# First loads spread over two hardware queues, the cast queue started later, half of a batch's q turned by DMA: one change to an attention and feed-forward kernel

## The chip, the core and the metric

One core of a Trainium2 chip. The metric is the device time of one execution in microseconds (us). Most executions of this kernel agree within 0.3%, and the change is worth about that much, so the timed runs are read together with traces, which resolve single instructions.

## The reference

```python
# q [8,16,384,64]; k, v [8,4,384,64]; 4 q heads share one k, v head (a "group")
scores = q @ k^T / sqrt(64)
attn   = softmax(scores) @ v
x      = attn with the heads side by side      # [3072, 1024]
h      = max(x @ w_in, 0)                      # w_in  [1024, 2048]
out    = (h * h) @ w_out                       # w_out [2048, 1024]
```

## The kernel before

The program records operations with a planned cost, and a loop picks for TensorE (PE) at each step what its own model says is ready. The order of instructions is thus fixed when the program is built; on the chip the engines follow it and wait by semaphores. Batches are called b0 to b7. To turn q, k or an attention output is to transpose it. A burst is the score matmuls and the one exp that reads them; the small exps are the 20 of b0. The cast queue is the DMA queue of gpsimd, whose loads turn f32 into bf16. While ScalarE (ACT) does the exps of one batch, PE fills in with the feed-forward of the batch before.

The parts that matter, with cuts marked:

```python
def first_loads():                       # f32, hardware queues
    for g0, g1 in ((0, 1), (1, HKV)):
        R.add("sync",   ... k_f32 groups g0..g1 ...)        # small k, then the bulk of k
    for n in range(2):
        R.add("scalar", ... q_f32 heads 2n, 2n+1 ...)       # both q loads on the other queue
...
def turn_q_dma(b, half):                 # transposes 8 of 16 heads by DMA, 384 KB
    R.add("sync", lambda e: e.dma_start_transpose(out=qT[b % 2][...], in_=q_st[b % NST][...]),
          ..., dma=f"turn_q{half}", cost=2.5, shared=8.0)
def turn_q_pe(b, g, banks, t0=0, t1=6):  # the same on PE: 6 transposes a group, then a DVE copy
    ...
# the cast queue (gpsimd), one long queue in this order:
load_q(0, 4, 8); ...identity...; load_v(0); load_q(0, 8, 12); load_q(0, 12, 16); load_w_in(0)
load_k(1); load_q(1, 0, 8); load_q(1, 8, 16); load_w_in(1); load_v(1)
load_w_in(2) ... load_w_in(7)
load_w_out(0, 0); load_w_out(0, 1); load_w_out(1, 0); load_w_out(1, 1)    # 1 MB each as read
# then k, q, v of b2
...
warm_up(22, 2.5)        # matmuls on zeros until the first k is there
...
# loop: turn_q = b0 and b1 on PE; from b2 on, k and q are turned by DMA
if turn_q and (b == 0 or pairs < 6 or x_done[0] == 8): ...   # candidate "turn"
```

The down projection of b0 uses the four w_out blocks in the order (0, 0), (0, 1), (1, 0), (1, 1). Each output tile of the first half starts with 8 matmuls from block (0, 0), then 8 from block (0, 1). I call (0, 1) the second block; its first use is the ninth w_out matmul of the program.

The softmax here doesn't subtract the row's maximum and nothing guards it: scores larger than these inputs give would overflow.

## Time and profile before

| | before |
|---|---|
| timed, first 3 runs | 430.74 us median (430.25 to 430.86) |
| profiled execution, span | 428.1 us |
| first exp on ACT | 6.59 us |
| first w_out matmul, ninth w_out matmul | 53.14 us, 54.87 us |
| second w_out block landed (landing events of the trace) | 49.84 us |

First the page of the kernel before: the span, the busy time of each engine, the clock that the record grants PE by fortieths of the span (9 is full), and the chain of work that ended last.

```profile
span 428.1 us, 7844 instructions
...
PE 423.2 (99%) x3467; PEld 232.2 (54%) x3467; DVE 158.8 (37%) x334; ACT 194.9 (46%) x194; POOL 55.1 (13%) x67
...
PEclk8999999999999999999999999999999999999999
...
PE 98%; DMA 1%; ACT 0%; DVE 0%; ACTq 0%; issue 0%
```

PE bounds the kernel. The Trainium skill ("Perfetto Trace Analysis", Identifying the Most-Contended Engine) says that the busy share of matmuls is no good measure of how close a kernel is to its limit, because pipelined instructions look smaller in the trace, and asks for the share of peak arithmetic and the busy share of weight loads instead; weight loads are at 54% here, so 99% is not "99% of the peak". For a kernel like this I read the starts of successive matmuls: a start later than the columns of the one before explain is time that PE lost. Some matmul records are missing from a few of the traces below; such a hole is one matmul long (0.22 us for a matmul of 512 columns) and is not a wait.

Next the timeline of the kernel before at its start: start, duration, engine, line, operation, tiles, count, and in brackets the engine's idle time before it with the releaser.

```profile
4.52 0.41 PE L302 MATMUL ps<-ident,q_st 128*128 128x128 bf16 x3
4.96 0.36 DVE L309 COPY qT<-ps 128x384 bf16<-128x384 bf16 x1 [0.38 <-PE ps L302]
5.30 0.51 ACT L551 CAST q_st<-q_f 128x384 bf16<-128x384 f32 x1 [0.97 <-DMA q_f<-in_q_dram]
5.96 0.33 PE L302 MATMUL ps<-ident,q_st 128*128 128x128 bf16 x3 [1.03 <-ACT q_st L551]
6.22 0.34 PE L328 MATMUL ps<-qT,kT 64*128 64x384 bf16 x2
6.59 2.43 ACT L338 ACTIVATE expT<-ps 128x768 bf16<-128x768 f32 x3 [0.78 <-PE ps L328]
...
9.81 0.82 PE L302 MATMUL ps<-ident,q_st 128*128 128x128 bf16 x6
...
11.43 0.52 PE L302 MATMUL ps<-ident,q_st 128*128 128x128 bf16 x6
```

ACT waits for the second q load until 5.30 us, PE stands for the second three transposes until 5.96, and the first score (L328) is behind them. The last two lines show the clock: six such transposes take 0.82 us at 9.81 and 0.52 us at 11.43. The table by stretches says the same in its column PEclk (here 0.52 of full between 8 and 10 us; the columns are busy time by engine with instruction counts, PEclk, DMA share, GB/s):

```profile
core 0: us, PE busy (x) PEld busy (x) DVE busy (x) ACT busy (x) POOL busy (x), PEclk, DMA share, GB/s
...
8.00:10.00 2.00, 2.00 (x17) 0.78 (x15) 0.92 (x2) 2.00 (x4) 2.00 (x4) 0.52 1.45 182
```

### The profile page before, as it was taken

The numbers are of one execution on the slowest core, as the hardware profiler recorded it, in microseconds if no ns is written. First come the engines' busy times: TensorE is split into PE (matmuls) and PEld (weight loads), VectorE is DVE, ScalarE is ACT, GpSimd is POOL, SyncE is SP. The second block draws the span as 40 slices with busy tenths as digits, with TensorE's granted clock in tenths as the row PEclk, the third lists the DMA queues.
The fourth block names the chain that finished last, engine by engine and source line by source line (L and its number), as shares of the span: only waits on it lengthen the run. The fifth ranks groups of instructions, "written<-read, shape, count | busy, mean of one in ns | idle before, by whom it ended". The sixth has DMA issues, their size and how long they took to land.

```text
span 428.1 us, 7844 instructions
## 1 busy us (share of the span) xinstructions
PE 423.2 (99%) x3467; PEld 232.2 (54%) x3467; DVE 158.8 (37%) x334; ACT 194.9 (46%) x194; POOL 55.1 (13%) x67
## 2 busy tenths in 40 slices
PE   7999999999999999999999999999999999999997
PEld 5565554565445654456554465645564465446544
DVE  2674432254223542325432253523342144214412
ACT  6947740557545675446765459550230033003300
POOL 8680011413040022004000000000000000000000
PEclk8999999999999999999999999999999999999999
DMA  9999999999599179369647410032001100110012
GB/s 180 193 198 204 187 195 190 236 152 130 90 188 166 20 133 141 98 145 145 64 80 140 89 45 18 16 92 81 37 2 49 73 26 2 49 73 26 1 66 83
DMA packets 95347, 43.90 MB, mean 103 GB/s; under 512 B 75728, under 2 KB 89296, under 8 KB 95312
## 3 DMA queue, kind: packets, MB, share of 16 engines
q0 software_dynamic: 36544, 17.44, 32.4%
q1 hardware_dynamic: 58224, 25.57, 28.0%
q8 instruction: 27, 0.44, 0.4%
q10 hardware_dynamic: 544, 0.39, 0.3%
q14 instruction: 8, 0.07, 0.1%
HBM read 35.65 MB, written 12.58 MB: 113 GB/s over the span
## 4 chain that ended last, share of the span: by engine, by line
PE 98%; DMA 1%; ACT 0%; DVE 0%; ACTq 0%; issue 0%
PE ps L431 40%; PE ps L480 39%; PE ps L374 9%; PE ps L349 7%; PE ps L328 1%; DMA q_f<-in_q_dram 1%; PE ps L302 1%; PE ps L407 0%; PE ps L286 0%; ACT expT L338 0%; DVE o_sb L389 0%; ACT q_st L551 0%; ACTq L218 0%; DVE y_sb L489 0%; DVE rinv L383 0%
## 5 line engine op out<-in xcount | busy, mean ns | idle before, releaser
L431 PE MATMUL ps<-xT,w_in_sb 128*128 128x384 bf16 x1024 | 175.0, 326 | 0.0
L480 PE MATMUL ps<-w_out_sb,h2T 128*128 128x512 bf16 (+2 forms) x784 | 172.0, 375 | 0.0
L359 ACT ACTIVATE expT<-ps 128x3072 bf16<-128x3072 f32 x42 | 114.4, 2725 | 57.7 <-PE ps L349 57.1
L431 PEld LDWEIGHTS ps<-xT,w_in_sb 128*128 128x128 bf16 x1024 | 96.8, 98 | 69.2 <-issue 6.4
L441 ACT ACTIVATE h2T<-hr 128x384 bf16<-128x384 f32 x128 | 64.3, 520 | 148.8 <-DVE hr L439 148.7
L480 PEld LDWEIGHTS ps<-w_out_sb,h2T 128*128 128x128 bf16 x784 | 73.8, 98 | 87.6 <-issue 5.4
L439 DVE TENSOR_SCALAR hr<-ps 128x384 f32<-128x384 f32 x128 | 71.1, 557 | 104.8 <-PE ps L431 104.8
L489 DVE COPY y_sb<-ps 128x512 f32<-128x512 f32 (+2 forms) x49 | 33.4, 681 | 127.4 <-PE ps L480 127.4
L374 PEld LDWEIGHTS ps<-v_aug,expT 128*128 128x128 bf16 x1152 | 39.8, 97 | 6.6 <-DVE o_sb L389 0.7
L374 PE MATMUL ps<-v_aug,expT 128*128 128x65 bf16 x1152 | 41.6, 193 | 0.1
L389 DVE TENSOR_TENSOR o_sb<-ps,rinv 128x384 bf16<-128x384 f32 x64 | 35.7, 558 | 2.2
L349 PE MATMUL ps<-qT,kT 64*128 64x512 bf16 (+1 forms) x336 | 34.6, 325 | 0.0
L349 PEld LDWEIGHTS ps<-qT,kT 64*128 64x128 bf16 x336 | 13.0, 94 | 20.7 <-issue 5.4
L383 DVE RECIPROCAL rinv<-ps 128x6 f32<-128x6 f32 x64 | 12.2, 190 | 24.1 <-PE ps L374 24.0
L338 ACT ACTIVATE expT<-ps 128x1024 bf16<-128x1024 f32 (+1 forms) x20 | 17.2, 941 | 1.7 <-PE ps L328 1.5
L263 POOL COPY v_aug<-v_st 128x768 bf16<-128x768 bf16 x8 | 6.7, 832 | 87.0 <-PE ps L374 71.9
L258 POOL COPY k_dup<-k_st 128x1536 bf16<-128x1536 bf16 x7 | 10.3, 1467 | 36.7 <-DMA k_st<-in_k_dram 36.7
L231 POOL DMA_DIRECT2D q_st<-in_q_dram x17 | 14.9, 888 | 0.9 <-POOLq L726 0.8
L205 POOL DMA_DIRECT2D k_st<-in_k_dram x7 | 5.3, 762 | 39.6 <-DMA qT<-q_st 39.6
L328 PE MATMUL ps<-qT,kT 64*128 64x384 bf16 (+2 forms) x48 | 8.0, 360 | 0.3 <-DVE qT L309 0.2
L241 POOL DMA_DIRECT2D w_in_sb<-in_moe_w_in_dram x8 | 7.1, 897 | 0.0
L224 POOL DMA_DIRECT2D v_st<-in_v_dram x8 | 6.3, 792 | 0.1
(26 smaller groups left out, 44.5 us busy)
## 6 DMA issues: line engine op xcount, KB each, us to landing
out_dram<-y_sb SPq DMA_DIRECT2D x47, 256.0 KB, 2.0
q_st<-in_q_dram POOLq DMA_DIRECT2D x14, 384.0 KB, 9.1
w_in_sb<-in_moe_w_in_dram POOLq DMA_DIRECT2D x8, 512.0 KB, 12.1
w_out_sb<-in_moe_w_out_dram POOLq DMA_DIRECT2D x4, 1024.0 KB, 27.0
v_st<-in_v_dram POOLq DMA_DIRECT2D x8, 192.0 KB, 10.6
k_st<-in_k_dram POOLq DMA_DIRECT2D x7, 192.0 KB, 4.3
q_st<-in_q_dram POOLq DMA_DIRECT2D x3, 192.0 KB, 5.2
xT<-o_sb SPq DMA_TRANSPOSE x28, 4.3
```

Source lines behind the costliest of these rows:

```text
L231: R.add("gpsimd", lambda g: g.dma_start(q_st[st][:, h0:h1, :], q[b, h0:h1].rearrange("h (p j) d -> p h (j d)", j=NJ)), writes=[("q_st", st ...
L328: mm = pe.matmul(ps[:, base + x, m * wide:(m + 1) * wide], kT[b % 2][64 * x:64 * x + 64, u, :], q_cols(b, u // NJ, x, c0, c0 + wide))
L338: R.add("scalar", lambda e: e.activation(dst, src, AF.Exp, scale=0.125), reads=keys, writes=[("expT", (b * NU + u) % NEX, t) for u, _, _ i ...
L349: m = pe.matmul(flat[:, k0 * HC + c0:k0 * HC + c1], kT[b % 2][64 * x:64 * x + 64, u + k0, :], q_cols(b, (u + k0) // NJ, x, c0, c1))
L359: R.add("scalar", lambda e: e.activation(dst, src, AF.Exp, scale=0.125), reads=keys, writes=[("expT", (n + m) % NEX, t) for m in range(2) ...
L374: m = pe.matmul(po[:, f - 6 * s2, 0:D + 1], w, v_aug[b % 2][:, g * NJ + j, 0:D + 1], start=(j == 0), stop=(j == NJ - 1))
L389: R.add("vector", lambda e: e.tensor_tensor(dst, srcv, rbv, ALU.mult), reads=[("bank", i), ("rinv", r)], writes=[("o_sb", o, s2)], cost=0.48)
L431: m = pe.matmul(bank(i)[:, 0:S], w_in_sb[:, kc, c * 128:(c + 1) * 128], xT[b % NXT][:, kc, :], start=(kc == 0), stop=(kc == NKC - 1))
L439: R.add("vector", lambda e: e.tensor_scalar_max(hr[r][:, :], bank(i)[:, 0:S], 0.0), reads=[("bank", i)], writes=[("hr", r)], cost=0.48)
L441: R.add("scalar", lambda e: e.activation(h2T[b % 2][:, c, :], hr[r][:, :], AF.Square), reads=[("hr", r)], writes=[("h2T", b % 2, c)], cost ...
L480: m = pe.matmul(bank(i)[:, 0:n], h2T[b % 2][:, c, i3 * 128:(i3 + 1) * 128], w_out_sb[:, c, c0:c1], start=(c == 0), stop=(c == NFC - 1))
L489: R.add("vector", lambda e: e.tensor_copy(ysl, bank(i)[:, 0:n]), reads=[("bank", i)], writes=[("y", yb)], cost=0.08 + n / 960)
```

## The change

It has four parts. (1) The second q load goes to the queue of the small k load, the bulk of k behind the first q load, and the cast queue begins after the identity is built. (2) The first score goes ahead of the second half of the first q turn, and the units of b0 are grouped so that the first two bursts need the first half only. (3) q groups 2 and 3 of b1 are turned by DMA, not on PE. (4) The scores of b2 are planned 3 us later.

```diff
     def first_loads():
-        for g0, g1 in ((0, 1), (1, HKV)): ... "sync" ... k
-        for n in range(2): ... "scalar" ... q
+        keys("sync", 0, 1)
+        queries("scalar", 0)
+        queries("sync", 1)
+        keys("scalar", 1, HKV)
...
-    R.ring["gpsimd"] = 4.0
-    load_q(0, 4, 8)
+    R.ring["gpsimd"] = 4.5
     ...identity...
+    load_q(0, 4, 8)
     load_v(0)
...
-    for group in ((0,), (1, 2), (3, 4), (5, 6), (7,), (8, 9), (10, 11)):
-        if len(group) == 2 and group[1] < NU - 1:
+    for group in ((0, 1), (2, 3), (4, 5), (6, 7), (8, 9), (10, 11)):
+        if 0 < group[0] < NU - 2:
...
-    turn_q += [... if (b, g) != (0, 0)]
+    turn_q += [... if (b, g) != (0, 0) and (b, g // 2, w) != (1, 1, "q")]
...
-    chores = []
+    chores = [([("q_st", 1, 2, 0)], lambda: turn_q_dma(1, 1))]
+    turned_g |= {(1, g, t) for g in (2, 3) for t in range(6)}
...
-        if turn_q and (b == 0 or pairs < 6 or x_done[0] == 8):
+        if turn_q and (b == 0 or ...) and (sc_q[0] != (0, 0) or w in "ka"):
...
-                t = max(R.when(reads=score_reads(b, u) + score_reads(b, u + 1)),
+                t = max(R.when(reads=score_reads(b, u) + score_reads(b, u + 1)) + 3.0 * (b == 2),
```

More of the change, by code (lines that the diff above doesn't have):

```diff
@@ L210, in first_loads, with keys, queries @@
     def first_loads():
-        for g0, g1 in ((0, 1), (1, HKV)):
-            R.add("sync", lambda e, g0=g0, g1=g1: e.dma_start(
+        def keys(eng, g0, g1):
+            R.add(eng, lambda e: e.dma_start(
                 k_f32[:, g0 * NJ:g1 * NJ, :].rearrange("p (g j) d -> p g (j d)", j=NJ),
                 k[0, g0:g1].rearrange("g (p j) d -> p g (j d)", j=NJ)),
-                writes=[("k_f32", g) for g in range(g0, g1)], dma=f"kf{g0}", cost=0.4 if g1 == 1 else 1.6, issue=0.4)
-        for n in range(2):
-            R.add("scalar", lambda e, n=n: e.dma_start(
+                writes=[("k_f32", g) for g in range(g0, g1)], dma=f"kf{g0}", cost=0.4 if g1 == 1 else 1.1, issue=0.4)
+        def queries(eng, n):
+            R.add(eng, lambda e: e.dma_start(
                 q_f32[:, 2 * n:2 * n + 2, :], q[0, 2 * n:2 * n + 2].rearrange("h (p j) d -> p h (j d)", j=NJ)),
                 writes=[("q_f32", n)], dma=f"qf{n}", cost=0.8, issue=0.4)
+        keys("sync", 0, 1)
+        queries("scalar", 0)
+        queries("sync", 1)
+        keys("scalar", 1, HKV)
     def load_v(b):
@@ L564, in bass_gqa_attention__then__ffn_squared_relu_kernel @@
     turn_q = [(0, 0, "a"), (0, 0, "c")]
-    turn_q += [(b, g, w) for b in range(2) for g in range(HKV) for w in "kq" if (b, g) != (0, 0)]
+    turn_q += [(b, g, w) for b in range(2) for g in range(HKV) for w in "kq"
+               if (b, g) != (0, 0) and (b, g // 2, w) != (1, 1, "q")]
     sc_q = [(0, n) for n in range(len(smalls))] + [(b, u) for b in range(1, B) for u in range(0, NU, 2)]
@@ L616, in bass_gqa_attention__then__ffn_squared_relu_kernel @@
             b, g, w = turn_q[0]
-        if turn_q and (b == 0 or pairs < 6 or x_done[0] == 8):
+        if turn_q and (b == 0 or pairs < 6 or x_done[0] == 8) and (sc_q[0] != (0, 0) or w in "ka"):
             src = [("k_dup", b, g, 0)] if w == "k" else [("q_st", b, g, h) for h in range(2) if w != "ac"[1 - h]]
```

## The prediction

> **What bounds the kernel now.** TensorE: the page gives PE 423.2 us busy of a 428.1 us span, and the chain of waits is 98% PE. By the starts of successive matmuls, none after 12 us is more than 0.25 us later than its predecessor's columns explain. A gain can come only from PE work taken away, or from PE time lost in the first 12 us.
>
> **The first 12 us.** In the timeline ACT's first q cast starts at 3.82 us, the second at 5.30 after 0.97 us idle (waiting for "DMA q_f"). PE stands 1.25 us (4.71 to 5.96) before the second three q transposes, and the first score is queued behind them, although kT and the first half of qT are ready by 5.32. First score 6.22 us, first exp 6.59. From there ACT is nearly solid until 24.6 us (20 bursts). The clock record shows one half-speed window, 8.08 to 11.49 us: the 3.41 us that the Trainium skill ("TensorE: Matmul & The Clock Gate", Part 1) gives for its activity monitor, right after the window with the stall.
>
> **What the change does.**
> 1. Loads. The second q load now follows the small k load (landed 3.23 us) instead of the first q load (3.79). The skill ("DMA: Bandwidth & Descriptors", Issuing engines are not separate DMA queues) says queues interleave on the same engines; here the bulk of k and the second q landed together, 5.11 and 5.28 us. From 0.17 MB per 0.5 us I estimate that this q lands near 4.4. The cast queue starts 0.5 to 0.7 us later; its first data landed at 6.43 and PE wants it at 7.8.
> 2. Order. The first score goes ahead of the second q half, and the first two bursts need the first half only. Estimate: score 5.4, first exp 5.75 instead of 6.59: -0.85 us. Bursts stay 20, of the same sizes. If the clock stays up, 0.2 more.
> 3. b1 q groups 2, 3: 12 PE transposes go, 0.056 us each: -0.67 us of PE work; two DVE copies of 0.56 us go too, off the path. One DMA transpose comes at about 18.5 us (source landed 18.41), wanted near 47 us. It delays weight loads (estimate 2 to 3 us, from the transposes at 84 to 93 us); only w_in block 1 (landed 21.0, wanted from 24.4) is near. Friction 0.2.
> 4. b2 scores later: no PE wait there now (first at 78.43 us, its last transpose landed 77.30). Insurance, about 0.
>
> **Sum.** -0.85 - 0.67 - 0.2 (clock) + 0.2 (friction) = -1.5 us, nearly all on the path, since PE is saturated afterwards. Predicted 429.2 us, 428.1 to 430.3. Faster by over 2%: 0.01; within 2%: 0.98; slower by over 2%: 0.01.
>
> **What would show it.** Second q cast near 4.5 us, first exp near 5.8, last small exp near 23.8; PE matmuls 3455 instead of 3467; 13 DMA transposes of q instead of 12; no PE gap at 24 to 31 us (weights) or 78 to 83 us (b2); the half-speed window moved or gone.
>
> **What would make it wrong.** The first q or k landing later in new company; PE or ACT waiting at 7 to 12 us for k group 1 or the cast loads, giving back the early start; the DMA transpose starving the weights; the clock window, which may fall differently from run to run.

## More of the kernel before

Last, two views of the kernel before for the weights: the DMA issue of the second w_out block (count, KB, us from issue to landing; it was issued at 25.48 us), and the timeline where PE first needs w_out (L480).

```profile
w_out_sb<-in_moe_w_out_dram POOLq DMA_DIRECT2D x1, 1024.0 KB, 24.4
```

```profile
52.48 0.82 PE L431 MATMUL ps<-xT,w_in_sb 128*128 128x384 bf16 x4
52.59 2.73 ACT L359 ACTIVATE expT<-ps 128x3072 bf16<-128x3072 f32 x1 [0.29 <-PE ps L349]
53.14 2.75 PE L480 MATMUL ps<-w_out_sb,h2T 128*128 128x512 bf16 x12
```

The twelve w_out matmuls run through. Their ninth starts at 54.87 us, and its block has been there since 49.84: five microseconds of room.

## The result

| | before | after |
|---|---|---|
| timed, 6 runs each of the same rounds | 430.50 us median (430.00 to 431.46) | 430.05 us median (429.48 to 431.12) |
| ratio, 95% interval | | 0.9989 (0.9971 to 1.0008) |
| profiled execution, span | 428.1 us | 427.8 us |
| first exp on ACT | 6.59 us | 6.06 us |
| PE at full clock from (clock record; the spacing of matmuls agrees) | 4.7 to 8.1, then 11.5 us | 13.4 us |
| second w_out block landed | 49.84 us | 54.21 us |
| first, ninth w_out matmul | 53.14, 54.87 us | 52.95, 54.68 us |

A ratio is the mean time of one kernel's fast runs over that of the other's of the same rounds, so it is not quite the ratio of the medians. Times "by the ratio" below are (ratio - 1) x 430 us. The change is -0.5 us by it, and its interval reaches past zero. I predicted -1.5 us with a range of 428.1 to 430.3; 430.05 lies inside it, near the upper edge.

The page of the changed kernel, the same lines as before:

```profile
span 427.8 us, 7819 instructions
...
PE 423.7 (99%) x3455; PEld 232.4 (54%) x3455; DVE 157.5 (37%) x332; ACT 194.9 (46%) x194; POOL 55.2 (13%) x67
...
PEclk9999999999999999999999999999999999999999
...
PE 98%; DMA 1%; ACT 0%; DVE 0%; issue 0%
```

The 12 transposes are gone (3455 instead of 3467), and PE's busy time is 0.5 us higher all the same, with PE at half clock until 13.4 us: a lesson in how little that number says. The timeline of the changed kernel at its start:

```profile
3.84 1.13 ACT L557 CAST q_st<-q_f 128x384 bf16<-128x384 f32 x2 [0.21 <-DMA q_f<-in_q_dram]
4.54 0.53 PE L308 MATMUL ps<-ident,q_st 128*128 128x128 bf16 x3
5.10 0.36 DVE L315 COPY qT<-ps 128x384 bf16<-128x384 bf16 x1 [0.49 <-PE ps L308]
5.52 0.82 PE L334 MATMUL ps<-qT,kT 64*128 64x384 bf16 x4 [0.45 <-DVE qT L315]
6.06 1.51 ACT L344 ACTIVATE expT<-ps 128x768 bf16<-128x768 f32 x2 [1.09 <-PE ps L334]
...
10.36 0.82 PE L308 MATMUL ps<-ident,q_st 128*128 128x128 bf16 x6
...
11.98 0.82 PE L308 MATMUL ps<-ident,q_st 128*128 128x128 bf16 x6
```

The loads did what was expected: the second q landed at 4.43 us (I had estimated 4.4) and ACT casts both without a pause to speak of. But six transposes still take 0.82 us at 11.98, where the kernel before was already at 0.52. The page's PEclk row shows 9 from the first slice on; that is no measurement, because the clock record of this execution has no entry before 13.39 us. The durations and spacings are what to trust. The last small exp of b0 ended at 24.74 us, against 24.62 before: the half microsecond of the start was gone by then in this execution.

The changed kernel's weights: the second w_out block (issued at 25.37 us), the new DMA turn (issued at 18.32 us), and PE's first use of w_out (now L486).

```profile
w_out_sb<-in_moe_w_out_dram POOLq DMA_DIRECT2D x1, 1024.0 KB, 28.8
...
qT<-q_st SPq DMA_TRANSPOSE x1, 12.3
```

```profile
52.29 0.82 PE L437 MATMUL ps<-xT,w_in_sb 128*128 128x384 bf16 x4
52.40 2.73 ACT L365 ACTIVATE expT<-ps 128x3072 bf16<-128x3072 f32 x1 [0.29 <-PE ps L355]
52.95 2.75 PE L486 MATMUL ps<-w_out_sb,h2T 128*128 128x512 bf16 x12
```

The block landed 4.4 us later than before (54.21 against 49.84). PE still ran through, but the room was 0.5 us (54.21 against 54.68), where it had been 5.

### The profile page after: what moved, and what is told of

It reads as the page before. It is cut to its first block, busy times and chain, and to the rows that moved or that the text cites. A ratio compares the mean times of both kernels' runs of the same rounds, so it can differ in the third digit from the quotient of the medians.

```text
span 427.8 us, 7819 instructions
## 1 busy us (share of the span) xinstructions
PE 423.7 (99%) x3455; PEld 232.4 (54%) x3455; DVE 157.5 (37%) x332; ACT 194.9 (46%) x194; POOL 55.2 (13%) x67
## 4 chain that ended last, share of the span: by engine, by line
PE 98%; DMA 1%; ACT 0%; DVE 0%; issue 0%
PE ps L437 40%; PE ps L486 39%; PE ps L380 9%; PE ps L355 7%; PE ps L334 2%; PE ps L308 1%; DMA k_f<-in_k_dram 1%; PE ps L413 0%; PE ps L292 0%; ACT expT L344 0%; DVE qT L315 0%; PE ps L544 0%; ACT k_dup L552 0%; DVE y_sb L495 0%
## 5 line engine op out<-in xcount | busy, mean ns | idle before, releaser
L486 PE MATMUL ps<-w_out_sb,h2T 128*128 128x512 bf16 (+2 forms) x784 | 172.1, 375 | 0.0
L486 PEld LDWEIGHTS ps<-w_out_sb,h2T 128*128 128x128 bf16 x784 | 73.7, 98 | 87.3 <-issue 5.1
```

Of the source, the lines that this page charges most:

```text
L486: m = pe.matmul(bank(i)[:, 0:n], h2T[b % 2][:, c, i3 * 128:(i3 + 1) * 128], w_out_sb[:, c, c0:c1], start=(c == 0), stop=(c == NFC - 1))
```

## The experiments

Twelve experiments ran, all with correct results, each timed in 5 rounds; one of them (after_again) is the changed kernel once more. "Fills" are warm-up matmuls on zeros in PE's gaps. Rows of the table with the same time before share a chip and the runs of the kernel before. "Full clock from" is the clock record's own time where it has an entry, and otherwise read from the spacing of neighbouring 128-column matmuls, 0.107 us at half and 0.056 us at full clock.

| kernel | median us (range) | before, same chip | by the ratio, us (95%) | full clock from, us | second w_out block landed; ninth w_out matmul, us |
|---|---|---|---|---|---|
| turns_late | 429.52 (428.98 to 430.14) | 430.11 | -0.65 (-1.29 to 0.00) | 9.4 | 53.90; 54.02 |
| start_only | 429.32 (428.62 to 429.85) | 430.11 | -0.90 (-1.55 to -0.30) | about 10 | 50.69; 54.27 |
| no_late | 430.83 (430.32 to 432.55) | 430.11 | +0.86 (+0.04 to +1.72) | 4.6 | 54.29; 54.33, waited |
| after_fill | 429.55 (428.99 to 431.66) | 430.11 | -0.43 (-1.33 to +0.47) | 6.0 | 55.10; 55.15, waited |
| start_late_fill | 428.76 (428.50 to 429.04) | 429.93 | -0.99 (-1.55 to -0.43) | 5.5 | 50.26; 53.39 |
| half_fill | 428.27 (427.85 to 428.77) | 429.93 | -1.46 (-2.06 to -0.86) | 4.6 | 52.41; 53.04 |
| aware_fill | 428.91 (428.30 to 430.62) | 429.93 | -0.69 (-1.46 to +0.09) | 4.6 | 54.88; 54.93 |
| before_fill | 429.19 (429.04 to 429.25) | 429.93 | -0.60 (-1.16 to -0.04) | 5.4 | 50.16; 53.94 |
| half | 429.00 (428.00 to 429.36) | 430.06 | -1.38 (-2.02 to -0.77) | about 10 | 53.35; 54.26 |
| start_dummy | 429.28 (428.76 to 430.46) | 430.06 | -0.65 (-1.33 to +0.04) | 13.3 | 54.42; 55.35 |
| after_again | 429.50 (429.32 to 429.92) | 430.06 | -0.56 (-1.07 to -0.04) | 5.4 | 54.48; 54.53, waited |
| defer_fill | 428.08 (427.59 to 428.36) | 430.02 | -1.85 (-2.62 to -1.08) | 5.0 | 50.87; 52.62 |

The intervals are about as wide as the effects.

**First theory (A):** the early start is worth little, since PE works at half clock then. **First rival (B):** the early start is worth its time, and the DMA turn takes it back by delaying weights.

### turns_late: parts 3 and 4 alone

```diff
 # before, plus
+    chores = [([("q_st", 1, 2, 0)], lambda: turn_q_dma(1, 1))]  ... and no PE turn of b1 groups 2, 3
+    ... + 3.0 * (b == 2)
```

> Before plus only the DMA turn of q groups 2, 3 of b1 and the later b2 scores; loads and order at the start as before. Theory A (the early start is worth little because PE runs at half speed in the first 8 to 13 us; the missing transposes are nearly the whole gain): -0.6 us against before, PE matmuls 3455, no new PE gap after 25 us. Theory B (the early start is worth its 0.5 to 0.85 us, and the DMA transpose takes it back by delaying the weight loads): 0 to +0.4 us, with a PE gap somewhere from 20 to 85 us.

-0.65 us, close to the 0.67 us of the transposes. B's 0 to +0.4 falls outside the interval, but only just (it ends at 0.00). The second w_out block landed at 53.90 us and its first matmul started at 54.02, without a wait: with the old start the room was already down to 0.1 us.

### start_only: parts 1 and 2 alone

```diff
 # before, plus
+ the new first_loads, load_q(0, 4, 8) behind the identity, the new groups, the gate on "c"
```

> Before plus only the new first loads, the cast queue behind the identity, the new groups and the first score ahead of the second q half; b1 turned on PE as before, b2 scores placed as before. Theory A: within 0.3 us of before, work lost by 30 us about equal to before's 12.1 us at a like clock. Theory B: -0.5 to -0.85 us. Both: first exp near 6.06 us instead of 6.59.

-0.90 us: A's number (within 0.3) falls as well, again at the edge of the interval. First exp 6.14 us, last small exp ended at 23.66 us. Alone, both parts measure about what I predicted for them (0.85 and 0.67); -0.90 and -0.65 make -1.55, and together they give -0.5. That points to a loss in their meeting. The times alone do not prove it: each of the three has an interval of 0.6 to 0.8 us to either side, so a difference of 1 us is not clear of them.

### no_late: the changed kernel without part 4

```diff
-                t = max(R.when(...) + 3.0 * (b == 2),
+                t = max(R.when(...),
```

> The changed kernel without the 3.0 on the b2 scores. In the changed kernel the first q transpose of b2 lands at 81.18 us, where before had it at about 76. The order of instructions puts the first b2 scores here 16 matmuls (2.6 us) earlier, at about 79.5 us. If the later placing is insurance only (as predicted): no difference to the changed kernel. If it pays for what the DMA turn costs the queue: a PE gap of 1.3 to 2 us at 79 to 82 us, and the kernel slower than before by about 1 us.

This execution had PE at full clock from 4.6 us, its last small exp ended at 22.47 us, and two waits appeared, both on DMA. The first lies in the part of the program that is instruction for instruction that of the changed kernel. The timeline of no_late (its seven matmuls before the wait are eight, see above):

```profile
50.89 1.67 PE L486 MATMUL ps<-w_out_sb,h2T 128*128 128x512 bf16 x7
54.33 1.04 PE L486 MATMUL ps<-w_out_sb,h2T 128*128 128x512 bf16 x4 [1.77 <-DMA w_out_sb<-in_moe_w_out_dram]
...
76.44 2.76 PE L437 MATMUL ps<-xT,w_in_sb 128*128 128x384 bf16 x16
...
80.11 0.82 PE L355 MATMUL ps<-qT,kT 64*128 64x512 bf16 x8 [0.90 <-DMA qT<-q_st]
```

PE reached w_out 2 us early and waited 1.77 us for the second block. The second wait, 0.9 us at 80 us for the first DMA turn of b2 (landed at 80.06 us; 76.03 in the kernel before), is the one that part 4 removes. It was smaller than the 1.3 to 2 us that I expected; the time is 1.3 us above the changed kernel's by the ratios, more than this one wait, with wide intervals and in other rounds. Part 4 is no insurance: it belongs to part 3.

### after_fill: keep PE fed at the start

```diff
-    warm_up(22, 2.5)
+    warm_up(25, 2.5)
+    # warm_up(6) after the first q turn, (2) after bursts 2 and 3, (3) after the turn of k group 1
```

> The changed kernel with warm-up matmuls in the gaps that PE has anyway: 25 instead of 22 at the start, 6 after the first q turn, 2 after the first two bursts, 3 after the turn of k group 1, 2 after the third burst; the order of the rest is the same. Theory A: the clock record turns to full speed before 10 us in most runs and stays, the last small exp ends near 24.2 instead of 24.74, and the time falls by 0.4 to 0.8 us below the changed kernel. Theory B (clock does not matter, ACT paces the start): 0 to +0.2 us.

The clock rose at 6.0 us and the last small exp ended at 22.96 us, more than A had asked for, and the time stayed that of the changed kernel: PE waited 2.25 us at 52.9 us (from the starts) for the second w_out block. So the half clock that A named is real, but lifting it did not bring the gain.

**Second theory (C):** the DMA turn puts the second w_out block at 54 to 55 us, and no execution can pass that point earlier, whatever the start gains. **Rival (D):** the gap at 52 us comes from the order or the fills.

### after_again: the changed kernel once more

No edit.

> The changed kernel as it is, on the chip of the other two: -0.3 to -0.6 us against before. If its profile falls on an execution whose clock comes up before 10 us, theory C has PE wait 1 to 2 us for the second w_out block; if it comes up at 13.4 us as in the first profile, no gap.

This gives the clearest evidence. The profile fell on an execution whose clock came up at 5.4 us. Its timeline at the start and at the first use of w_out:

```profile
5.46 0.50 PE L334 MATMUL ps<-qT,kT 64*128 64x384 bf16 x4 [0.45 <-DVE qT L315]
5.84 6.68 ACT L344 ACTIVATE expT<-ps 128x768 bf16<-128x768 f32 x8 [0.51 <-PE ps L334]
...
10.43 0.51 PE L308 MATMUL ps<-ident,q_st 128*128 128x128 bf16 x6 [0.16 <-DVE qT L315]
...
50.22 0.82 PE L437 MATMUL ps<-xT,w_in_sb 128*128 128x384 bf16 x4
50.33 2.73 ACT L365 ACTIVATE expT<-ps 128x3072 bf16<-128x3072 f32 x1 [0.29 <-PE ps L355]
50.88 1.89 PE L486 MATMUL ps<-w_out_sb,h2T 128*128 128x512 bf16 x8
...
54.53 1.04 PE L486 MATMUL ps<-w_out_sb,h2T 128*128 128x512 bf16 x4 [1.76 <-DMA w_out_sb<-in_moe_w_out_dram]
```

Six transposes take 0.51 us here against 0.82 us in the first profile at the same place. PE reaches w_out at 50.88 us instead of 52.95: 2.1 us ahead with the same program. It then waits 1.76 us and goes on at 54.53, where the first profile was at 54.68. The spans are 427.7 and 427.8 us. Two microseconds of luck at the start changed the total by 0.1.

### start_late_fill: fills, but no DMA turn

```diff
 # after_fill, with b1 turned on PE as before (no entry in chores, full turn_q)
```

> after_fill without the DMA turn: q groups 2, 3 of b1 are turned on PE again. In after_fill PE reached the second w_out block at 53.1 us and waited until 55.10 us. Theory C (the DMA turn delays the weight queue by about 4.4 us, the second w_out block lands at 54 to 55 us instead of 50 to 51, and whatever the start gains beyond that is given back there): the block lands near 51, no PE gap at 52 us, the time falls by 1 to 1.6 us below after_fill although PE has 0.67 us more to do, about -1.7 us against before. Rival D (the gap comes from the order or the fills, the DMA turn is a clean -0.67): 0.7 us slower than after_fill.

The block landed at 50.26 us, there was no wait, and the time fell 0.6 us below after_fill's by the ratios although PE had 0.67 us more to do. C holds in sign and in the trace. The gain was under the 1 to 1.6 us that I had written, and the two kernels ran on different chips, so by time alone it is not shown.

### half and half_fill: half of the DMA turn

```diff
-  (b, g // 2, w) != (1, 1, "q")          # groups 2 and 3 by DMA
+  (b, g, w) != (1, 3, "q")               # group 3 only
-    chores = [([("q_st", 1, 2, 0)], lambda: turn_q_dma(1, 1))]
+    chores = [([("q_st", 1, 3, 0)], turn_q3_dma)]     # 4 heads instead of 8
```

> The changed kernel, no fills, with only group 3 of b1 turned by DMA and group 2 on PE: 0.33 us of PE work comes back, half of the DMA transposes go. Theory C (the two parts are worth 0.9 and 0.65 us alone, but together PE meets the second w_out block, which the whole DMA turn puts at 54 to 55 us): the block lands near 52.4 us as in half_fill, no PE gap there, -1.1 to -1.4 us against before, 0.6 to 0.9 us faster than after_again although PE has more to do. Rival (the parts lose against each other in the first 12 us): 0.3 us slower than after_again.

> after_fill with only group 3 turned by DMA (half the bytes), group 2 on PE. Theory C: the second w_out block lands near 52.5 us, PE waits 0 to 0.4 us there, time 1.2 to 1.9 us below after_fill, about -1.8 us against before. Rival D: 0.33 us slower than after_fill.

Without fills: -1.38 us, and on the same chip 0.5 us below after_again by the medians (429.00 and 429.50; 0.8 by the ratios, where 0.6 to 0.9 was expected) although PE does 6 transposes more. The second block took 26.9 us from its issue, between the 24.4 us of before and the 28.8 us of the changed kernel:

```profile
w_out_sb<-in_moe_w_out_dram POOLq DMA_DIRECT2D x1, 1024.0 KB, 26.9
```

That profile had a late clock (about 10 us) and no wait. With fills the clock was up at 4.6 us, PE came to w_out at 51.31 us, and the timeline of half_fill shows no wait there:

```profile
51.31 2.75 PE L486 MATMUL ps<-w_out_sb,h2T 128*128 128x512 bf16 x12
```

-1.46 us, 1.0 below after_fill by the ratios, on another chip. C had said 1.2 to 1.9 below, D 0.33 above.

### start_dummy: the cost of the DMA turn without its benefit

```diff
 # parts 1, 2, 4; all of b1 turned on PE; and
+    chores = [([("q_st", 1, 2, 0)], turn_twice)]   # the same DMA transpose into an unread tile
```

> The new start and the later b2 scores, all of b1 turned on PE, and beside it the DMA turn of q groups 2, 3 into a tile that nobody reads: the cost of the DMA turn without its benefit. Theory C: its second w_out block lands at 54 to 55 us and sets the time; about the time of after_again (within 0.3 us), -0.2 to -0.5 us against before, with a PE gap at 52 to 54 us where the clock comes up early. Rival: a DMA transpose off the path costs nothing; -0.9 us against before, as the start alone.

The second block landed at 54.42 us (50.69 in start_only, with the same start and no DMA turn in b1), so the added transfer puts it there even when nobody reads its result. The time, -0.65 us, lies between the two forecasts and its interval holds both. The profile had a clock that rose at 13.3 us, so PE came late and did not wait.

### aware_fill: tell the scheduler

The kernel's own model plans the second w_out block at 48.0 us in the kernel before and 48.5 us in the changed one (the later cast queue): when the DMA turn is recorded, the weight loads already stand in the model's queue, and its cost moves only later loads.

```diff
-   dma=f"wi{i}", cost=2.65
+   dma=f"wi{i}", cost=2.65 + 5.5 * (i == 2)
```

> after_fill with one number of the scheduler's own model changed: weight loads from the third w_in block on are planned 5.5 us later, as they land. The DMA work is the same; PE gets a score pair and an attention-value group (1.9 us) ahead of the third w_out use. Theory C: the block still lands at 54 to 55 us, the PE gap there falls from 2.25 us to under 0.5 us, time 1.5 to 2 us below after_fill, about -2 us against before. Rival D: no difference.

The wait at 52 us went to nothing, as C said. The total did not follow: in the profiled execution, the slowest of its six, PE waited for the fourth block (landed at 69.06 us), as the timeline of aware_fill shows:

```profile
65.77 1.67 PE L486 MATMUL ps<-w_out_sb,h2T 128*128 128x512 bf16 x7
...
69.11 0.61 PE L486 MATMUL ps<-w_out_sb,h2T 128*128 128x512 bf16 x2 [1.66 <-DMA w_out_sb<-in_moe_w_out_dram]
```

The fourth block had landed at 65.79 us in after_fill. The new order of PE also moved transfers (the output transposes at 58.29 and 65.46 us in after_fill were issued at 56.08 and 63.29 here), so this is a new wait at a block that came 3.3 us later, in one execution. My -2 us was a miss.

### before_fill: fills alone

```diff
 # before, plus
+    warm_up(25, 2.5); warm_up(11) between the two halves of the first q turn
```

> Before with 25 warm-up matmuls instead of 22 at the start and 11 between the two first q turns; order of the rest the same. If the clock in the first 12 us is worth its time to before too, and its weights land with room (49.84 us against a use at 54.9): first exp still near 6.6 us, full speed from 6 to 8 us on in most runs, -0.5 to -1.2 us against before with no gap at 52 us. If ACT paces the start regardless of the clock: within 0.2 us.

-0.60 us, with all five runs between 429.04 and 429.25 where the kernel before spread from 428.99 to 430.36 on that chip. This suggests that a good part of the spread of the kernel before is the clock at the start; the trace of one execution each cannot show it. On the same chip and at like clocks (full from 5.4 and 5.5 us) start_late_fill was 0.4 us below before_fill by the medians (428.76 against 429.19): so much is left of the new start, with part 4, when both have fills.

### defer_fill: the whole DMA turn, other transposes later

The DMA transposes of the first two attention outputs of b1 were issued at 41 and 47 us in the changed kernel (38.9 and 45.4 in after_fill), while weights were landing, and nothing reads them before about 77 us.

```diff
 # after_fill, in turn_o_dma:
-            reads=[("o_sb", o, 0), ("o_sb", o, 1)],
+            reads=[("o_sb", o, 0), ("o_sb", o, 1)] + [("w_out", 0, 1)] * (b == 1 and g < 2),
```

> after_fill (whole DMA turn, fills) with the first two DMA transposes of the b1 attention output, issued at 41 and 47 us and not read before 77 us, made to wait for the second w_out block. If it is DMA transposes in general that hold the weight queue up: the second w_out block lands at 51 to 52 us instead of 55.1, the PE gap at 52 us goes from 2.25 to under 0.5 us, and a gap of 0 to 0.7 us may come up at 66 us (fourth w_out block, landing near 65.8); 1.3 to 2 us below after_fill, about -1.7 us against before. If only the b1 q turn itself matters: the block still lands near 55 and nothing changes.

The second block took 25.1 us from its issue and landed at 50.87 us, and PE went through. The DMA issue of that block and the timeline of defer_fill (the first w_out record is missing in it, as said above):

```profile
w_out_sb<-in_moe_w_out_dram POOLq DMA_DIRECT2D x1, 1024.0 KB, 25.1
```

```profile
50.23 0.82 PE L438 MATMUL ps<-xT,w_in_sb 128*128 128x384 bf16 x4
...
51.11 2.54 PE L487 MATMUL ps<-w_out_sb,h2T 128*128 128x512 bf16 x11
53.48 1.28 PE L380 MATMUL ps<-v_aug,expT 128*128 128x65 bf16 x36
```

The fourth block landed at 63.55 us, and no wait came up at 66. -1.85 us: 428.08 us median, span 425.8, the lowest of all versions, ahead of the kernel before and, by the ratios, of the changed one; half_fill (428.27, another chip) is not told apart from it. The whole q turn is still there, so the late block was not the work of the q turn alone: it and the output transposes behind it make it together.

## Why the prediction was right or wrong

- **Bound by PE, gains only from the first 12 us and from PE work taken away:** right as a description of the kernel before. It hid an assumption: that the bound stays where it is when PE gets faster.
- **Loads and order, -0.85 us:** the path was right, the agreement in size partly luck. The second q landed at 4.43 us (estimate 4.4). The first exp came at 5.72 to 6.32 us in the eleven traces with the new start (median 6.01), where I had 5.75. Alone the part measured -0.90 (-1.55 to -0.30), but the first exp came only 0.6 us earlier by that median (6.59 before), and with fills on both sides 0.4 us was left (start_late_fill against before_fill).
- **Clock, -0.2 us "if it stays up":** the step was real but not to be had by this change. The changed kernel's PE came to full clock at 13.4 us in one profile and at 5.4 us in another. The Trainium skill ("TensorE: Matmul & The Clock Gate", Part 1) says that the activity window runs free of the kernel's start; records 3.41 us long and such jumps between executions agree with that. In all six profiles with fills the clock was up by 6.0 us, without fills in three of eight (in one of these it fell back). I have not shown what decides it within an execution.
- **12 transposes, -0.67 us:** in line with the runs; -0.65 alone (-1.29 to 0.00).
- **The step that failed:** "It delays weight loads (estimate 2 to 3 us ...); only w_in block 1 ... is near. Friction 0.2." The delay of 2 to 3 us was well estimated for the w_in blocks: the last of them landed 3.0 us later in turns_late than before (41.07 against 38.04), and PE did not wait for one. But the delay was 4.4 us at the second w_out block (4.1 us in turns_late, where the loads at the start are as before; 0.9 us in start_only, which I put down to the later cast queue), and that block was near. The last microsecond came behind the w_in blocks, where the first two output transposes of b1 share the engines with w_out; with these held back the block was in time (defer_fill). With the start's gain PE arrives up to 2 us earlier, just as the block comes 4.4 us later. The friction term of 0.2 was thus too small: -1.55 for the parts alone against -0.5 together would make it about 1 us, a size that the intervals do not secure; the waits of 1.77, 1.76 and 2.25 us in the traces of no_late, after_again and after_fill are what is shown. I had checked the room of one block against the old arrival of PE, when both were about to move towards each other.
- **b2 scores later, "insurance, about 0":** no wait in the changed kernel, as said, but for the wrong reason. Without the part PE waits 0.9 us at 80 us for the b2 turn, which the DMA turn had pushed from 76.03 us in the kernel before to 80.06 (81.18 in the changed kernel).
- **The range held the result,** but not for the reason given: the wait at the second w_out block was not foreseen. In the execution with a slow start (after) there was no wait at all, and no gain from the start either; in the one with a fast start (after_again) the wait took the gain back. That both ended within the range was luck.

Open: whether halving the DMA turn and deferring the output transposes add up; how much of defer_fill is due to the fills; and what share of the executions of the changed kernel reach the wait (two traces of it show one with and one without), and so how much of the missing 1 us is this wait and how much is the clock at the start.

## What to carry to other kernels

Two improvements that each measure well can fail together when one brings the consumer forward and the other holds a producer back: before adding them, list for each load its landing, its first use and the room between, and move both ends. In a kernel whose order was fixed by a model, check that the model charges a new transfer to the transfers that are already planned behind it. And when executions differ at the start and the totals do not, look for the point where they become equal; what PE waits for there sets the time.

## What the Trainium skill lacked or had wrong

- "DMA: Bandwidth & Descriptors", DMA Transpose (X-bar): no cost of a transpose beside other traffic. With one DMA transpose of 384 KB in flight from 18.3 to 30.5 us among cast loads, the last w_in block landed 3.0 us later (turns_late 41.07 against before 38.04 us), and the second w_out block, which two output transposes delay too, 4.1 us later (53.90 against 49.84); at the 197 GB/s that the loads of the kernel before moved from 18 to 31 us, as many bytes of load would be 2.0 us (an estimate from these numbers). With fills the block landed at 50.26 us without the transpose, 52.41 with half of it and 55.10 with all of it. The rule (Rules for kernel authors) that a transpose next to ordinary DMAs needs nothing is about safety; for time it isn't so here. What the loads lose beyond the bytes is not settled, but one trace shows a part: in the kernel before, with two output transposes in flight, the DMA engines moved 9 to 12 GB/s from 48.25 to 48.85 us, and in defer_fill, which holds these two back, never under 171 GB/s from 46 to 52 us (slices of 0.15 us).
- "TensorE: Matmul & The Clock Gate", Part 1: it speaks of about 3.4 us at half clock. A start of short matmuls, transposes and waits stayed there until 13.4 us in one execution and 5.4 us in another of the same program, and in the kernel before it fell back for 3.41 us after it had come up. Short warm-up matmuls in PE's gaps had it up by 6.0 us in six of six profiles.
- "TensorE: Matmul & The Clock Gate", Part 1, warns that the clock events of a trace can be unreliable, but not of this case: a clock record without an entry at the start reads as full clock in the table by stretches and is none. Six transposes at 11.98 us took 0.82 us instead of 0.51 us, with the first entry of the record at 13.39 us.
